# Moving four loads and one block of sums, and adding epsilon as a sum over pairs, in a fused attention and feed-forward kernel

## The chip, the cores and the metric

The kernel runs on one core of one Trainium2 chip. The metric is the device time of one execution in microseconds (us), the median of three runs. Five engines matter: TensorE (PE in the profile; its weight loads are PEld), VectorE (DVE), ScalarE (ACT), GpSimd (POOL) and SyncE (SP), whose only work here is to issue DMAs. Each engine takes its instructions strictly in the order in which they were written, and waits on semaphores for the others. DMAs issued by SP and ACT go to one kind of queue (q1, q10 in the profile), those issued by GpSimd to another (q0).

## The reference

```python
def _attn_ref(q, k, v, tau):
    q_n = q / (np.linalg.norm(q, axis=-1, keepdims=True) + 1e-06)
    k_n = k / (np.linalg.norm(k, axis=-1, keepdims=True) + 1e-06)
    scores = np.matmul(q_n, k_n.transpose(0, 1, 3, 2)) / tau
    scores = scores - np.max(scores, axis=-1, keepdims=True)
    attn = np.exp(scores)
    attn = attn / (np.sum(attn, axis=-1, keepdims=True) + 1e-09)
    return np.matmul(attn, v).astype(np.float32)

def _moe_ref(x, w_in, w_out):
    h = x @ w_in
    g = np.maximum(0.01 * h, h)
    return (g @ w_out).astype(np.float32)
```

q, k and v have shape (8, 12, 448, 64): 8 batches, 12 heads, 448 positions, 64 numbers each, in float32; tau is 0.1. The attention's output, (3584, 768) after its heads are put side by side, goes through w_in (768 x 2048), a leaky maximum, and w_out (2048 x 768).

## The kernel before, in words

**Slots, quads, units.** Work is cut into *slots* of normalisation. For the first two batches a slot is q and k of one pair of heads: slots 0 to 5 are batch 0, slots 6 to 11 batch 1. From slot 12 (`OLD`) on, slots come in twos that make a *unit*: the even one is q of two pairs of heads, the odd one k of the same two. Slots 12 and 13 are unit 0, slots 14 and 15 unit 1, slots 16 and 17 unit 2. A *quad* is four heads, so two slots of the first batches; quads 0 to 2 are batch 0, quads 3 to 5 batch 1.

**A slot's chain.** `load_qk(s)` loads it (lines 128 to 151; SP's queue but for slots 0 and 1, whose k is issued by ACT). `squares(s)` multiplies it with itself on GpSimd (L201, L208). `sums(s)` adds up the squares on VectorE (L216, L222). `roots(s)` takes the root as a logarithm and an exponential on ScalarE (L229, L230). `normalise(s)` adds epsilon on VectorE (L238), takes the reciprocal (L239) and multiplies it in (L245 for units, L255 for the first slots). `transposes(s)` turns the result: for the first slots on TensorE (L269) with a copy by VectorE (L310); for units on VectorE (L291), and when a unit's second slot is turned, six DMAs on SP's queue (L300) put it in place as qkT. `hold(x)` is a tiny copy on GpSimd (L585) that makes GpSimd wait for `normalise`, so that it doesn't start the next squares too soon. The pool of loaded tiles has four buffers, so slot s + 4 uses the buffer of slot s.

**Scores and products.** `key_tiles` (called by `scores`) makes score tiles of 128 keys by two heads on TensorE (L331) and ScalarE takes their exp (L340); `quad_tiles` does it for units (L402, exp L408). `totals(j)` sums a quad's exps over the keys with matmuls (L351) and takes the inverse on ScalarE as a logarithm and an exponential (L362, L363); `products(j, e)` multiplies them with the values (L351 too); `scale(j, e)` on VectorE (L382) writes the scaled result to xT. `attend(j)` is `totals`, two `products` and two `scale`. A quad's values come by `load_v(j)` (L162) and `load_v_rem(b)` (L170, last 64 positions of a batch's heads), both issued by GpSimd; for units it is `load_vq(g)` (L188).

**Feed-forward.** `first(c, m)` multiplies xT of chunk c with one 128-wide slice of w_in (L476), and ScalarE writes it to hT (L485); there are 16 slices. `second(c, ts, half)` multiplies hT with one half of w_out (L507); VectorE copies the result out (L518) and SP stores it (L527). One call of `second` is an *output group*. The weights are loaded by GpSimd: `load_w_in(i)`, i from 0 to 3 (L107), and `load_w_out(half)` (L113).

**The order.** All of it is written out by hand, in one list that fixes every engine's order. A loop over batch 0's slots (lines 621 to 676) comes first; a straight part (lines 687 to 744) does quad 2, the first groups of `first` and the normalisation of slots 6 to 10; a loop over `opened` (lines 750 to 790) does batch 1's remaining score tiles, quads 3 and 4, and five output groups, one for each of its five rounds; then *visits* (lines 829 to 882) do three quad tiles each, with further groups. In a round of `opened` the third number is the slot whose sums, roots and normalisation are due: 11, 12, 13, 14. In round 2 of the old order, for instance, that is slot 13, whose turning completes unit 0.

**PSUM banks.** PSUM's eight banks are dealt by age (`banks`, lines 78 to 88): a tile gets the bank that was dealt longest ago. A tile of two heads takes two banks. TensorE waits if the engine that reads the bank's former content isn't done.

**DMA semaphores.** The framework deals eight semaphores in turn to SP's and ACT's DMAs, and eight to GpSimd's. A DMA that is issued waits for the DMA eight before it of its kind to have landed, and the issuing engine waits with it.

Of the kernel before, what the change touches and what calls it, by code (L numbers as in the profile page):

```python
# [8 lines left out]
F32 = mybir.dt.float32  # L9
BF16 = mybir.dt.bfloat16  # L10
AF = mybir.ActivationFunctionType
ALU = mybir.AluOpType
AX = mybir.AxisListType
# [3 lines left out]
def kernel(  # L17
# [10 lines left out]
    nc = tc.nc  # L28
# [96 lines left out]
            x[:, 512:896].rearrange("p (h t d) -> p h t d", h=2, d=D),  # L125
        )

    def load_qk(s, engs=(nc.sync, nc.sync)):
        if s >= NSLOT:
            return  # L130
        whole = ldp.tile([128, 14 * D], F32, name="qk_h")
        if s >= OLD:
            u, which = divmod(s - OLD, 2)
            for w, pair in enumerate(UNITS[u][1]):
                b, h0 = pair // NPAIR, 2 * (pair % NPAIR)
                nc.sync.dma_start(
                    out=whole[64 * w : 64 * w + 64],
                    in_=(q, k)[which][b, h0 : h0 + 2].rearrange("h (p t) d -> (h p) (t d)", t=14),
                )
            raw[s] = whole  # L140
            return
        b, h0 = s // NPAIR, 2 * (s % NPAIR)
        q_h, k_h = halves(whole)
        engs[0].dma_start(out=q_h[:, :, 0:3], in_=main(q, b, h0, 2))
        engs[1].dma_start(out=k_h, in_=main(k, b, h0, 2))
        for i, (x, eng) in enumerate(zip((q, k), engs)):
            eng.dma_start(
                out=q_h[64 * i : 64 * i + 64, :, 3],
                in_=x[b, h0 : h0 + 2, MAIN:S].rearrange("h p d -> p h d"),
            )  # L150
        raw[s] = (q_h, k_h)
# [5 lines left out]
    def load_v(j):  # L157
        if j >= B * NQ:
            return
        b, jj = divmod(j, NQ)  # L160
        vb[j] = vbp.tile([128, 4, 3, D], BF16, name="v_b")
        gp.dma_start(out=vb[j], in_=main(v, b, 4 * jj, 4))  # L162

    def load_v_rem(b, heads=range(4)):
        if b >= B:
            return
        r = v[b, :, MAIN:S].rearrange("(j g) p d -> g p j d", g=4)
        for g in heads:
            lo = 64 * (g // 2)
            gp.dma_start(out=vrb[b % 2][lo : lo + 64, :, g], in_=r[g])  # L170
# [9 lines left out]
    def load_vq(g):  # L180
        js = GROUPS[g]
        nh = 2 * len(js)
        vq[g] = vqp.tile([128, 4, 7, D], BF16, name="vq")
        for w in range(2):
            b, jj = divmod(js[w % len(js)], NQ)
            h0 = 4 * jj + (2 * w if len(js) == 1 else 0)
            rows = slice(64 * w, 64 * w + 64)
            gp.dma_start(  # L188
                out=vq[g][rows, 0:nh],
                in_=v[b, h0 : h0 + nh].rearrange("h (p x) d -> p h x d", x=7),  # L190
            )
# [3 lines left out]
    def squares(s, engs=(gp, gp)):  # L195
        if s >= NSLOT:
            return
        sq = sqp.tile([128, 14 * D], F32, name="sq")
        if s >= OLD:
            sqs[s] = sq  # L200
            gp.tensor_tensor(sq, raw[s], raw[s], op=ALU.mult)  # L201
            return
        sqs[s] = halves(sq)
        for x, y, eng in zip(raw[s], sqs[s], engs):
            if eng is nc.scalar:
                nc.scalar.activation(y, x, func=AF.Square)
            else:
                eng.tensor_tensor(y, x, x, op=ALU.mult)  # L208
# [17 lines left out]
    def roots(s):  # L226
        if s >= NSLOT:
            return
        nc.scalar.activation(ss[s], ss[s], func=AF.Ln, bias=tiny)  # L229
        nc.scalar.activation(ss[s], ss[s], func=AF.Exp, scale=0.5)  # L230

    qn = {}

    def normalise(s):
        if s >= NSLOT:
            return
        r = smp.tile([128, 14], F32, name="r")
        nc.vector.tensor_tensor(ss[s], ss[s], eps, op=ALU.add)  # L238
        nc.vector.reciprocal(r, ss[s])  # L239
        if s >= OLD:  # L240


            qn[s] = qnp.tile([128, 7, D, 2], BF16, name="qn")
            t, n = ("(m e)", "(e m)")[s % 2], 2
            nc.vector.tensor_tensor(  # L245
                qn[s].rearrange("p m d e -> p m e d"),
                raw[s].rearrange(f"p ({t[1:-1]} d) -> p m e d", e=n, d=D),
                r.rearrange(f"p {t} -> p m e", e=n).unsqueeze(3).to_broadcast([128, 7, 2, D]),
                op=ALU.mult,
            )  # L250
            return
        qn[s] = qnp.tile([128, 7, 2, D], BF16, name="qn")
        for x, lo, hi, r0 in ((raw[s][0], 0, 4, 0), (raw[s][1], 4, 7, 8)):
            nt = hi - lo
            nc.vector.tensor_tensor(  # L255
                qn[s][:, lo:hi],
                x.rearrange("p h t d -> p t h d"),
                r[:, r0 : r0 + 2 * nt].rearrange("p (h t) -> p t h", h=2)
                .unsqueeze(3).to_broadcast([128, nt, 2, D]),
                op=ALU.mult,  # L260
            )
# [286 lines left out]
            work[c].pop(0)[1]()  # L548

    load_qk(0, (nc.sync, nc.scalar))  # L550
    load_qk(1, (nc.sync, nc.scalar))
    load_qk(2)
    load_qk(3)
    tiny = cpool.tile([128, 1], F32, name="tiny")
    nc.vector.memset(tiny, 1e-18)
    eps = cpool.tile([128, 14], F32, name="eps")
    nc.vector.memset(eps, 1e-6)
    warm = pep.tile([128, 2 * S], BF16, name="pe")[:, 0:512]
    nc.vector.memset(warm, 1.0)  # L559
    ones = cpool.tile([128, 32], BF16, name="ones")  # L560
# [60 lines left out]
    for s in range(NPAIR):  # L621
        j = s // 2 - 1 if s >= 2 else None
        even = s % 2 == 0
        n = s + 2 if 0 < s < NPAIR - 2 else None
        last = s == NPAIR - 1
        if s == 1:
            roots(2)
        scores(s, (0,))
        if j is not None and not even:
            products(j, 1)  # L630
        scores(s, (1,))
        fill(2)
        if n:
            sums(n, (0,))
        if not last:
            normalise(s + 1)
            load_qk(s + 5)
        if late:
            scale(late.pop(), 1)
        if j is not None and not even:  # L640
            scale(j, 0)
        if last:
            load_v(s // 2 + 1)
            load_v_rem(1)
            load_w_out(0)
        else:
            hold(qn[s + 1][:, 6, 0, 0:1])
        squares(s + 3)
        if s == 0:
            sums(2)  # L650
            load_v_rem(0, range(2, 4))
        if not even and not last:
            load_v(s // 2 + 1)
        if s != 1 and not last:
            load_w_in(max(s - 1, 0))
        if n:
            sums(n, (1,))
        scores(s, (2,))
        if not even or s == 0:
            fill(2)  # L660
        if n and not even:
            roots(n)
        if not even:
            scores(s, (3,))
        if j is not None and even:
            totals(j)
        if not last:
            transposes(s + 1)
        if j is not None and even:
            products(j, 0)  # L670
        if not even or s == 0:
            fill(2)
        if n and even:
            roots(n)
        if j is not None and not even:
            late.append(j)
# [24 lines left out]
    for m in range(2):  # L701
# [36 lines left out]
    transposes(s + 3)  # L738
    roots(s + 4)
    normalise(s + 4)  # L740
    load_qk(s + 7)
    hold(qn[s + 4][:, 6, 0, 0:1])
    squares(s + 5)
    feed_groups(0, 1)
# [3 lines left out]


    opened = [  # L750
        (0, [(2, 0), (2, 1), (2, 2)], 5),
        (None, [(3, 0), (3, 1), (3, 2)], 6),
        (None, [(4, 0), (4, 1), (3, 3)], 7),
        (1, [(4, 2), (5, 0), (5, 1)], 8),
        (None, [(5, 2), (5, 3)], None),
    ]
# [1 line left out]
    b = 1  # L758
    queue += work[0]
    costs = [BLOCK + (ATTEND if at is not None else 0) for at, _, _ in opened[1:] + [(2, 0, 0)]]  # L760
    for i, (at, tiles, ahead) in enumerate(opened):
        share = (sum(g[0] for g in queue[:-1]) + sum(costs[i:])) / (len(opened) - i) - costs[i]
        if at is not None:
            attend(b * NQ + at)
            if at == 0:
                load_v(b * NQ + 2)
            else:
                load_vq(0)
        key_tiles([(b * NPAIR + p, ki) for p, ki in tiles])
        done = 0  # L770
        s = b * NPAIR + ahead if ahead else NSLOT
        sums(s)
        roots(s)
        if i < 2:
            if i == 1:
                cost, fn = queue.pop(0)
                fn()
                done += cost
            transposes(NPAIR + 4 + i)
        if s < NSLOT:  # L780
            normalise(s)
            if s >= OLD:
                transposes(s)
            load_qk(s + 3)
            hold(qn[s][:, 6, 0, 0:1])
            squares(s + 1)
        while len(queue) > 1 and (i == len(opened) - 1 or done + queue[0][0] / 2 <= share):
            cost, fn = queue.pop(0)
            fn()
            done += cost  # L790
    load_qk(OLD + 6)
    sums(OLD + 3)
    squares(OLD + 4)
# [137 lines left out]
```

## Time and profile before

| what | us |
|---|---|
| median of 3 runs | 422.59 (422.2 to 422.63) |
| the profiled execution, device time | 422.44 |
| its span in the profile | 420.7 |
| TensorE busy | 410.2 |
| ScalarE busy | 254.7 |
| VectorE busy | 223.2 |
| GpSimd busy | 115.2 |
| first matmul starts | 1.51 |

The profile's page lists each engine's busy time, and groups of instructions by line, with the idle time of the engine just before them and what ended it. The trace also gives a timeline: start, duration, engine, line, operation, what is written and read, how many instructions in a row were merged (x12), and in brackets the idle time before the row with what released it, for instance `[1.30 <-DMA v_b<-in_v_dram]`. Times in the text without another word are microseconds from the span's start. A DMA's landing is its issue plus the time that the trace gives for issue to landing.

### The profile page before, as it was taken

How to read it: one execution, taken by the hardware profiler on the slowest of the kernel's cores; microseconds unless marked ns; L12 is line 12 of the kernel's file. 1: busy time of each engine (PE TensorE's matmuls, PEld its weight loads, DVE VectorE, ACT ScalarE, POOL GpSimd, SP SyncE). 2: the span in 40 equal slices, each digit the busy share in tenths (PEclk: the TensorE clock that was granted, in tenths of full speed). 3: DMA queues.
4: the chain of work that ended last, by engine and by line, in shares of the span. 5: the costliest groups of instructions: out<-in, count | busy, mean ns of one | idle time of the engine just before them, and what ended most of it. 6: DMA issues, size and time to landing. Idle time of an engine off the chain costs nothing.

```text
span 420.7 us, 11326 instructions
## 1 busy us (share of the span) xinstructions
PE 410.2 (98%) x4779; PEld 212.5 (51%) x4797; DVE 223.2 (53%) x383; ACT 254.7 (61%) x430; POOL 115.2 (27%) x149
## 2 busy tenths in 40 slices
PE   8898999999999999999999999999999999999996
PEld 3234555444455555554445555554445555654563
DVE  6885887785668745776564964565511312110021
ACT  3895885678847686658866687657764454104300
POOL 3868262533234132413331432123010000000000
PEclk9999999999999999999999999999999999999999
DMA  6899999767376953674465574543441100010021
GB/s 171 163 232 232 212 243 185 176 185 208 63 186 153 242 132 67 158 200 130 77 161 161 117 197 110 138 125 92 88 89 43 74 38 3 37 76 0 2 75 75
DMA packets 41906, 53.82 MB, mean 128 GB/s; under 512 B 12544, under 2 KB 32256, under 8 KB 41856
## 3 DMA queue, kind: packets, MB, share of 16 engines
q1 hardware_dynamic: 25536, 40.85, 34.1%
q0 software_dynamic: 15488, 11.80, 19.5%
q8 instruction: 37, 0.61, 0.6%
q10 hardware_dynamic: 832, 0.46, 0.4%
q14 instruction: 13, 0.11, 0.1%
HBM read 45.61 MB, written 11.01 MB: 135 GB/s over the span
## 4 chain that ended last, share of the span: by engine, by line
PE 92%; DMA 4%; DVE 2%; issue 1%; POOL 0%; SPq 0%; ACT 0%; POOLq 0%; DVEq 0%
PE ps L507 35%; PE ps L476 35%; PE ps L427 9%; PE ps L402 7%; PE ps L351 2%; DMA qk_h<-in_k_dram 2%; PE ps L576 2%; DMA v_b<-in_v_dram 2%; PE ps L331 1%; PE ps L269 1%; DVE qn L255 1%; POOL sq L208 0%; DVE ss L222 0%; DVE ss L238 0%; DVE osb L518 0%
## 5 line engine op out<-in xcount | busy, mean ns | idle before, releaser
L507 PE MATMUL ps<-w_out_sb,hT 128*128 128x384 bf16 x896 | 151.5, 327 | 0.2 <-DVE xT L382 0.2
L476 PE MATMUL ps<-xT,w_in_sb 128*128 128x384 bf16 (+1 forms) x753 | 149.8, 353 | 0.9 <-issue 0.2
L408 ACT ACTIVATE pe<-ps 128x896 bf16<-128x896 f32 x126 | 108.9, 916 | 41.6 <-PE ps L402 41.6
L507 PEld LDWEIGHTS <-hT 128*128 128x128 bf16 x896 | 85.3, 98 | 64.7 <-issue 10.4
L476 PEld LDWEIGHTS <-w_in_sb 128*128 128x128 bf16 x768 | 73.0, 98 | 73.5 <-issue 8.4
L485 ACT ACTIVATE hT<-ps 128x384 bf16<-128x384 f32 (+1 forms) x128 | 67.9, 548 | 63.0 <-PE ps L476 62.4
L518 DVE COPY osb<-ps 128x384 f32<-128x384 f32 (+1 forms) x56 | 30.8, 550 | 106.1 <-PE ps L507 100.4
L201 POOL TENSOR_TENSOR sq<-qk_h 128x896 f32<-128x896 f32 x36 | 60.4, 1679 | 4.8 <-DMA qk_h<-in_k_dram 2.6
L585 POOL CAST seen<-qn 128x1 f32<-128x1 bf16 x46 | 8.4, 184 | 176.2 <-DVE qn L245 161.8
L245 DVE TENSOR_TENSOR qn<-qk_h,r 128x896 bf16<-128x896 f32 x36 | 42.5, 1181 | 1.2
L340 ACT ACTIVATE pe<-ps 128x896 bf16<-128x896 f32 x42 | 36.0, 917 | 6.3 <-PE ps L331 6.3
L216 DVE TENSOR_REDUCE ss<-sq 128x14 f32<-128x896 f32 x36 | 37.5, 1041 | 2.5 <-POOL sq L201 2.5
L402 PE MATMUL ps<-qkT 64*32 64x448 bf16 x1008 | 37.0, 353 | 0.0
L238 DVE TENSOR_TENSOR ss<-ss,eps 128x14 f32<-128x14 f32 x48 | 11.0, 228 | 46.8 <-ACT ss L230 46.4
L452 DVE TENSOR_TENSOR xT<-ps,rb 128x448 bf16<-128x448 f32 x32 | 18.4, 617 | 21.9 <-PE ps L427 20.8
L291 DVE STREAM_TRANSPOSE tt<-qn 128x448 f32<-128x448 f32 x36 | 29.5, 820 | 0.9
L427 PE MATMUL ps<-pe,vq 64*32 64x448 bf16 x1008 | 27.0, 349 | 0.0
L229 ACT ACTIVATE ss<-ss,tiny 128x14 f32<-128x14 f32 x48 | 14.7, 306 | 19.1 <-DVE ss L216 16.7
L402 PEld LDWEIGHTS <-qkT 64*32 64x32 bf16 x1008 | 13.3, 91 | 20.0 <-issue 15.4
L208 POOL TENSOR_TENSOR sq<-qk_h 128x384 f32<-128x384 f32 (+1 forms) x21 | 20.1, 974 | 10.0 <-DMA qk_h<-in_k_dram 10.0
L427 PEld LDWEIGHTS <-vq 64*32 64x32 bf16 x1008 | 14.6, 93 | 7.9 <-issue 0.3
L576 PE MATMUL ps<-pe 128*128 128x512 bf16 x50 | 16.5, 454 | 1.6 <-DVE pe L559 1.5
(52 smaller groups left out, 216.0 us busy)
## 6 DMA issues: line engine op xcount, KB each, us to landing
qk_h<-in_q_dram SPq DMA_DIRECT2D x36, 224.0 KB, 4.1
qk_h<-in_k_dram SPq DMA_DIRECT2D x36, 224.0 KB, 4.4
out_dram<-osb SPq DMA_DIRECT2D x20, 384.0 KB, 2.6
qkT<-tt SPq DMA_DIRECT2D x72, 56.0 KB, 2.7
qkT<-tt SPq DMA_DIRECT2D x36, 112.0 KB, 2.9
vq<-in_v_dram POOLq DMA_DIRECT2D x16, 224.0 KB, 4.9
w_in_sb<-in_moe_w_in_dram POOLq DMA_DIRECT2D x4, 768.0 KB, 10.1
w_out_sb<-in_moe_w_out_dram POOLq DMA_DIRECT2D x2, 1536.0 KB, 20.7
```

Source lines behind the costliest of these rows:

```text
L201: gp.tensor_tensor(sq, raw[s], raw[s], op=ALU.mult)
L216: nc.vector.tensor_reduce(ss[s], sqs[s].rearrange("p (t d) -> p t d", d=D), axis=AX.X, op=ALU.add)
L245: nc.vector.tensor_tensor(qn[s].rearrange("p m d e -> p m e d"), raw[s].rearrange(f"p ({t[1:-1]} d) -> p m e d", e=n, d=D), r.rearrange(f" ...
L291: nc.vector.transpose(out=to.rearrange(("p g (c m) -> p m g c", "p g (m c) -> p m g c")[which], m=7), in_=qn[s].bitcast(F32).rearrange("p ...
L340: nc.scalar.activation(out=dst, in_=sc[:, :, :S], func=AF.Exp, scale=inv_tau)
L402: nc.tensor.matmul(out=sc[32 * strip : 32 * strip + 32, a, :S], lhsT=x[rows, c0 : c0 + 32], rhs=x[rows, 0:S], start=True, stop=True,)
L408: nc.scalar.activation(out=pq[u, i], in_=sc[:, :, :S], func=AF.Exp, scale=inv_tau)
L427: nc.tensor.matmul(out=po[32 * strip : 32 * strip + 32, w, :S], lhsT=weights, rhs=pq[us[x if two else 0], i][rows, a, :], start=(i == 0), ...
L476: nc.tensor.matmul(out=pm[:, :n], lhsT=w_in_sb[:, kt, m * 128 : (m + 1) * 128], rhs=xT[c // 2][:, kt, c0 : c0 + n], start=(kt == 0), stop= ...
L485: nc.scalar.activation(out=hT[c][:, m, :n], in_=pm[:, :n], func=AF.Prelu, alpha=0.01)
L507: nc.tensor.matmul(out=po2[:, :HALF], lhsT=hT[c][:, m, ts * 128 : (ts + 1) * 128], rhs=w_out_sb[:, m, half * HALF : (half + 1) * HALF], st ...
L518: nc.vector.tensor_copy(out=o[:, half * HALF : half * HALF + cut], in_=po2[:, :cut])
```

## The change

The first slots' loads: slot 1's last piece of k is issued by SP in place of ACT. Epsilon: the root is written next to a constant 1e-6, so that pairs (root, epsilon) lie side by side in one of three tiles, and `normalise` sums each pair, where it added two tiles. Batch 0's loop: quad 2's values are loaded in round 2 where it was round 3; in the last round the first half of w_out is loaded, and slot 8 squared, ahead of quad 3's values. The `opened` loop: quad 3's sums and products move from round 0 to round 2. In rounds 0 and 1 a slot's normalisation stays ahead of the output groups; in rounds 2 and 3 it comes behind the group. Loads 13, 14 and 15 are called one round later than they were (load 13 in round 0 in place of the straight part, and so on), and round 3 calls loads 16 and 17; `load_vq(0)` moves to the end of round 3.

In the order of instructions this comes to the following. TensorE: the sums and products of quad 3 (48 matmuls) move behind the second output group and slot 11's transposes; the first output group now stands ahead of slot 9's score tiles. SP: load 15 moves from before the first six DMAs of L300 to behind them; the first store follows it, ahead of loads 16 and 17; loads 13 and 14 keep their places. GpSimd: the loads named above, and `load_vq(0)` behind the squares of slot 15. VectorE: three memsets in place of one, and quad 3's two scalings behind slot 12's turning.

```diff
-    def load_qk(s, engs=(nc.sync, nc.sync)):
+    def load_qk(s, engs=(nc.sync, nc.sync), rem_engs=None):
...
-        for i, (x, eng) in enumerate(zip((q, k), engs)):
+        for i, (x, eng) in enumerate(zip((q, k), rem_engs or engs)):
...
         nc.scalar.activation(ss[s], ss[s], func=AF.Ln, bias=tiny)
-        nc.scalar.activation(ss[s], ss[s], func=AF.Exp, scale=0.5)
+        nc.scalar.activation(norms[s % 3][:, :, 0], ss[s], func=AF.Exp, scale=0.5)
...
-        nc.vector.tensor_tensor(ss[s], ss[s], eps, op=ALU.add)
-        nc.vector.reciprocal(r, ss[s])
+        nc.vector.tensor_reduce(r, norms[s % 3], axis=AX.X, op=ALU.add)
+        nc.vector.reciprocal(r, r)
...
-    load_qk(1, (nc.sync, nc.scalar))
+    load_qk(1, (nc.sync, nc.scalar), (nc.sync, nc.sync))
...
-    eps = cpool.tile([128, 14], F32, name="eps")
-    nc.vector.memset(eps, 1e-6)
+    norms = []
+    for i in range(3):
+        norms.append(cpool.tile([128, 14, 2], F32, name=f"norms{i}"))
+        nc.vector.memset(norms[i], 1e-6)
...
         if last:
-            load_v(s // 2 + 1)
-            load_v_rem(1)
             load_w_out(0)
...
-        if not even and not last:
-            load_v(s // 2 + 1)
-        if s != 1 and not last:
+        if s in (1, 2):
+            load_v(s)
+        if last:
+            load_v(NQ)
+            load_v_rem(1)
+        elif s != 1:
             load_w_in(max(s - 1, 0))
...
     normalise(s + 4)
-    load_qk(s + 7)
     hold(qn[s + 4][:, 6, 0, 0:1])
...
     opened = [
-        (0, [(2, 0), (2, 1), (2, 2)], 5),
+        (None, [(2, 0), (2, 1), (2, 2)], 5),
         (None, [(3, 0), (3, 1), (3, 2)], 6),
-        (None, [(4, 0), (4, 1), (3, 3)], 7),
+        (0, [(4, 0), (4, 1), (3, 3)], 7),
...
         if at is not None:
             attend(b * NQ + at)
-            if at == 0:
-                load_v(b * NQ + 2)
-            else:
-                load_vq(0)
+        if i == 0:
+            load_v(b * NQ + 2)
...
-        if s < NSLOT:
+
+        def prepare():
             normalise(s)
             if s >= OLD:
                 transposes(s)
-            load_qk(s + 3)
+            for n in ((s + 2,), (s + 2, s + 3))[i == 3]:
+                load_qk(n)
             hold(qn[s][:, 6, 0, 0:1])
             squares(s + 1)
+
+        if i < 2:
+            prepare()
         while len(queue) > 1 and (i == len(opened) - 1 or done + queue[0][0] / 2 <= share):
...
             done += cost
+        if i in (2, 3):
+            prepare()
+        if i == 3:
+            load_vq(0)
```

## The prediction

> **What bounds the kernel now.** I read four views in this order: the page's head, TensorE's timeline, the timeline of all engines from 52 to 86 us, and the DMA queue's own timeline with the bytes moved per microsecond. Times are microseconds of the one profiled execution: span 420.7, device time 422.44, which is 0.15 under the median of the three runs shown (422.59).
>
> ```profile
> span 420.7 us, 11326 instructions
> ...
> PE 410.2 (98%) x4779; PEld 212.5 (51%) x4797; DVE 223.2 (53%) x383; ACT 254.7 (61%) x430; POOL 115.2 (27%) x149
> ```
>
> TensorE (PE) is busy for 98%, and its work doesn't change: the same 9,596 rows, in which one block has moved. So the time can only move by TensorE's idle time, 10.5 us, of which 1.5 lie before its first matmul and 3.6 behind its last. What is left is 5.4, nearly all before 90 us. The two largest waits:
>
> ```profile
> 14.77 0.55 PE L331 MATMUL ps<-qkT 64*128 64x448 bf16 x4 [0.81 <-ACT ss L230]
> ...
> 36.76 0.75 PE L351 MATMUL ps<-pe,v_b 128*32 128x448 bf16 x12 [1.30 <-DMA v_b<-in_v_dram]
> ```
>
> From 38.4 to 73 TensorE never waits, yet several producers there finish only just before it comes, so an order that brings it sooner to something may open a wait. The rows that decide this case, out of the timelines of the engines (start, duration, engine, line; the rows between them are left out):
>
> ```profile
> 54.76 0.31 ACT L229 ACTIVATE ss<-ss,tiny 128x14 f32<-128x14 f32 x1 [0.36 <-DVE ss L222]
> 55.83 1.16 DVE L255 TENSOR_TENSOR qn<-qk_h,r 128x512 bf16<-128x512 f32 x2
> 57.83 0.57 PE L269 MATMUL ps<-id,qn 128*128 128x128 bf16 x7
> ...
> 62.29 1.11 SPq L136 DMA_DIRECT2D qk_h<-in_k_dram  x2
> 74.06 3.79 SPq L300 DMA_DIRECT2D qkT<-tt  x6
> 78.35 1.15 SPq L136 DMA_DIRECT2D qk_h<-in_q_dram  x2
> ...
> 81.43 1.07 DVE L216 TENSOR_REDUCE ss<-sq 128x14 f32<-128x896 f32 x1
> 82.54 0.31 ACT L229 ACTIVATE ss<-ss,tiny 128x14 f32<-128x14 f32 x1 [2.74 <-DVE ss L216]
> 82.80 1.68 POOL L201 TENSOR_TENSOR sq<-qk_h 128x896 f32<-128x896 f32 x1 [2.17 <-DMA qk_h<-in_q_dram]
> 83.00 0.90 ACT L408 ACTIVATE pe<-ps 128x896 bf16<-128x896 f32 x1
> 83.54 0.79 PE L402 MATMUL ps<-qkT 64*32 64x448 bf16 x16
> ```
>
> See three things. Slot 10's transposes (57.83) follow the end of its normalised values (56.99) by 0.84 only. Slot 15's load is issued at 62.29, and 16's, behind the six DMAs of L300, at 78.35; the squares of 16 (82.80) wait for it, 4.45 after its issue. And slot 15's roots (82.54) stand in ScalarE's queue ahead of the first exp of the quad tiles (83.00 to 83.90). The third quad tile uses that exp's two PSUM banks again, so it starts at about 84.0: 16 matmuls took 0.79 where 0.56 is usual.
>
> **The change, part by part.** Third quad's values: the load of quad 2's values moves in GpSimd's queue from 29.89 (landed 36.71, 6.82 later) to 22.80, in front of the second load of input weights. The slowest load of values near it took 8.4, so it lands by 31.2, and TensorE asks at 35.46: minus 1.30. Next late are those weights: landed 33.3 before, now behind 0.2 MB more (about 1.2 at the 0.16 MB per us that this queue moves there), so 34.5 against a need at 36.8. Nothing.
>
> Epsilon: 48 adds of two operands (L238, 0.228 mean, 0.17 the usual one) become 48 sums over pairs of 28 elements. The nearest rows are that 0.17 and the 0.278 of a sum of 128 elements; I take 0.18, VectorE being half idle, and nothing on TensorE's path. The gain is elsewhere: three of the old adds took 0.85, 0.64 and 1.39, and each ended as GpSimd's running multiplication did, while sums over 384 and 512 elements beside such multiplications took their usual time. Only the one at 10.81 is on the path: it ended at 11.66, the multiply L255 ran to 13.13, two sums and the copy L310 to 14.72, and TensorE started at 14.77. A sum ends at 11.0; the multiply has two operands and still waits for GpSimd's end at 11.63, or at about 11.3 if GpSimd too is earlier. That is 0.3 to 0.6 out of the 0.81; I take 0.4. The Trainium skill's page "SBUF — State Buffer", section "SBUF: two separate sides", says that VectorE and GpSimd take a shared port pair as an exclusive lock held for the whole instruction, an operation with two SBUF inputs among those that need it. By that rule the lock isn't removed, only handed to the next multiply; the trace agrees (2.00 and 2.02 for the pair of L255 at 27.25 and 51.43, where 1.16 is usual), and the sum by it is the 0.3. Against this, two more memsets stand before the one that TensorE's first matmul waits for (eps to it: 0.13 start to start). Between 0.06 and 0.26; I take 0.1. Start-up together: minus 0.3.
>
> Slot 1's last piece of k goes from ScalarE's queue to SP's: it waited there from 2.62 to 5.38, and ScalarE's first square started at 6.02 though q had landed at 3.83. Roots of slot 0 could come 1.3 sooner, but VectorE has a sum there that waits for GpSimd until 6.99, and TensorE warms up until 9.40 in any case. On SP the k of slot 2 then waits for a landing at 5.34 in place of 4.25; its squares start at 9.8. Nothing.
>
> Output weights ahead of later values: POOL issues the first half at about 33.5 in place of 37.39, and its queue no longer has quad 3's values (landed 45.05, remainders 45.9, the load ahead of them 44.16: 1.74) in front. It landed at 60.9 and was used at 61.95. Now output groups begin before key tiles (0.69) and quad 3's sums (2.38), at 58.83 of the old clock, which the other terms shift to 58.2. Landing by the 1.74 alone is 59.2; the queue also stood nearly empty from 31.5 to 33.2 (8 of 589 packets in one us), which the earlier values fill: 58.0. Between 0 and 1.0 late; I take 0. Quad 3's values land behind them, at about 60, and are wanted at 66; the four remainder loads hold POOL from about 37 to 40, before slot 6's hold. Nothing.
>
> Fourth quad's sums later (attend(3), 2.38): TensorE comes to slot 10's transposes at 55.52 of the old clock, not 57.83. What they wait for doesn't move with the block: ScalarE is free for slot 10's roots at 54.39 (end of L485), 0.37 sooner than it did them. From the roots' start to the ends of the two multiplies it took 1.76 and 2.23: 56.16 and 56.63. The last three of seven transposes follow the second, and end at 56.9 in place of 55.91: plus 1.0. Low end 0.6 (first multiply alone), high end 1.6 (VectorE lost 0.86 at 51.43 beside GpSimd's squares of slot 10, which depend on a load that landed at 51.8).
>
> The moved block also puts its two scalings (L382) on VectorE behind slot 12's normalisation. The third output group takes a PSUM bank that the first scaling frees. From the copy at 65.21 to the end of slot 12's transpose was 3.51, the scaling is 0.62, the sum 4.2 from the second group's end; TensorE arrives after 0.39 + 2.38 + 0.69 = 3.46. Plus 0.75 (0.3 to 1.0).
>
> Norms behind output groups, and loads with them: slot 13's normalisation now follows the third group's copy, and load 15 (62.29 before) follows on SP the six L300 of the unit that slot 13 completes. Count from the third group's end, 71.11 before. Copy, add, reciprocal, multiply, transpose: 0.04 + 0.47 + 0.20 + 0.27 + 1.26 + 0.65 = 2.89, and 0.13 to L300: 3.02. Six L300 3.79: load 15 at 6.9. Squares 4.45 later, as for slot 16: 11.35, and 1.67 long. Sum starts at 13.05, roots 1.11 later (81.43 to 82.54): 14.16; from there to the end of the exp 1.36: 15.5. Third quad tile at 15.6, where it was 84.0 - 71.11 = 12.9. Plus 2.7. A quiet load took 3.0 to land; with 0.57 between its two DMAs that gives 0.9 less, and load 19's squares came 4.89 behind its issue, 0.4 more: 1.8 to 3.1. Behind it ScalarE holds the exp and the logs of quad 5, but the tile covers them. Slot 15's own transposed tiles then land at 24.4 on this count and are wanted at 24.7. The values for group 0 move from 75.14 to behind squares 15 and are wanted at 108. Loads 13 and 14 keep their place on SP.
>
> Sum: -1.30 - 0.3 + 1.0 + 0.75 + 2.7 = +2.85, so 422.44 + 2.85 = 425.3.
>
> **The rivals.** (1) Faster: the waits at the values and in start-up go, and no new one opens: -1.6, 420.8. It needs three covers at once in slots 10, 12 and 15, but one decides: slot 15's squares must start within 8.6 of the third group's end, not 11.35, so load 15 must be issued 2.7 sooner. SP's order speaks against it (six L300, then load 15); for it speaks only that landing times here run from 2 to 10. (2) Slot 15 is in time, the two smaller waits remain: -1.6 + 1.75 = +0.15, 422.6: the change buys nothing. (3) The output weights are late by the whole 1.0 too: 426.3. For it: the queue's tail was starved from 55.5 to 58.5 (39 packets a us against 160) by loads of 3.5 KB rows beside it. The Trainium skill's page "DMA: Bandwidth & Descriptors", section "Queues, rings and completion order", says each DMA engine goes round robin between queues by packet; the trace agrees (153 and 153 packets in the microsecond from 46), and by it a queue loses to larger packets just as seen, wherever its transfer still has a tail at 55.
>
> **How the numbers follow.** Forecast, slot 15 late: 0.64. Rival 1: 0.12. Rival 2: 0.10, half of it within 0.2% (0.84 us, about what a measurement of this kernel can tell from no change), 0.04 slower, 0.01 faster. Rival 3: 0.14. Slower 0.64 + 0.14 + 0.04 = 0.82, same 0.05, faster 0.13. Low ends of all terms (0.6, 0.3, 1.8) give 423.5, high ends with the weights 422.44 - 1.6 + 1.6 + 1.0 + 3.1 + 1.0 = 427.5, unlikely together. 422.5 to 426.5 leaves out rival 1, part of rival 2 and the top of rival 3, some 0.19; the forecast's own range is 423.5 to 426.5.
>
> **What would show it.** No wait for v_b at the third quad; L238 at 0.17 to 0.28 and never over 0.4; a wait of about 1 before slot 10's transposes (L269); one of about 0.75 before the third output group, released by L382; load 15 on SP right behind the first six L300; GpSimd's squares of slot 15 waiting for that load; ScalarE's roots of slot 15 idle for over 4 us; and TensorE idle for some 2.7 in the middle of visit 0, released by L408. I am wrong if load 15 has landed before GpSimd comes to it, or if the quad tile finds its banks free.

## The result, and the profile after

The changed kernel takes 429.06 us (median of 4 runs, 428.32 to 429.84) against 422.61 before: a ratio of 1.0155, 95% interval 1.0133 to 1.0177. It is slower, as forecast, but by 6.5 us and not by 2.7; 429.06 lies outside the range of 422.5 to 426.5. The profiled execution took 429.49 us, with a span of 427.7, 7.0 longer than the span before. One run of the epsilon kernel below (1484.48 us) and one of the kernel before that ran beside the last four kernels (704.23 us, mean clock 0.559) were slow ones and are in no median or ratio here.

The head of the profile and the row of the granted clock, of the kernel after:

```profile
PE 412.0 (96%) x4779; PEld 213.0 (50%) x4797; DVE 222.3 (52%) x385; ACT 255.2 (60%) x430; POOL 116.7 (27%) x149
...
PEclk9999999969999999999999999999999999999999
```

The same row of the clock before, and the sixth output group in TensorE's timeline before:

```profile
PEclk9999999999999999999999999999999999999999
...
84.26 2.77 PE L507 MATMUL ps<-w_out_sb,hT 128*128 128x384 bf16 x16
```

TensorE's busy time has grown by 1.8 although its work is the same, and one slice of the 40, the one from about 86 us on, was granted a clock of only 0.6. Before, every slice of that row read 9. Next, TensorE's own timeline after (start, duration, engine, line, operation, instructions; idle time ahead and what ended it):

```profile
14.49 0.55 PE L331 MATMUL ps<-qkT 64*128 64x448 bf16 x4 [0.62 <-ACT norms L230]
...
35.04 0.74 PE L351 MATMUL ps<-pe,v_b 128*32 128x448 bf16 x12
...
53.81 0.94 PE L331 MATMUL ps<-qkT 64*64 64x448 bf16 x12
55.64 0.81 PE L269 MATMUL ps<-id,qn 128*128 128x128 bf16 x7 [0.89 <-DVE qn L255]
...
69.65 2.76 PE L507 MATMUL ps<-w_out_sb,hT 128*128 128x384 bf16 x16 [0.81 <-DVE xT L382]
72.34 0.75 PE L351 MATMUL ps<-pe,ones 128*32 128x448 bf16 x12
...
84.47 0.38 PE L402 MATMUL ps<-qkT 64*32 64x448 bf16 x8
88.34 0.57 PE L402 MATMUL ps<-qkT 64*32 64x448 bf16 x8 [3.48 <-ACT pe L408]
88.84 5.30 PE L507 MATMUL ps<-w_out_sb,hT 128*128 128x384 bf16 x16
```

The wait for quad 2's values is gone (35.04), and the three waits of the forecast are there: 0.89 at slot 10's transposes, 0.81 at the third output group, 3.48 at the third quad tile. What is new is the row behind it: an output group of 16 matmuls takes 5.30, where the five ahead of it took 2.76 or 2.77, as it did itself before. The clock says why, here in windows of the trace after (stretch, its length, busy time and instructions of PE, PEld, DVE, ACT and POOL, then the granted clock, the DMA share and GB/s):

```profile
87.00:88.00 1.00, 0.00 (x0) 0.00 (x0) 0.42 (x2) 0.97 (x3) 0.00 (x0) 0.68 0.99 280
88.00:89.00 1.00, 0.66 (x9) 0.25 (x9) 0.99 (x1) 0.97 (x3) 0.83 (x1) 0.50 1.07 359
...
94.00:95.00 1.00, 0.86 (x25) 0.37 (x26) 0.78 (x3) 0.43 (x1) 0.00 (x0) 0.91 0.35 84
```

TensorE's last matmul ends at 84.85 (84.47 + 0.38). Some 2.5 later, while it still waits, the clock falls to 0.50, and it stays there through the whole output group. A difference table of the two profiles, by the start of the same block of TensorE's work, shows where the 7.0 arose:

| block of TensorE | before | after | behind by |
|---|---|---|---|
| input group behind quad 2's products (L476) | 38.38 | 36.66 | -1.72 |
| input group behind slot 9's transposes (L476) | 53.69 | 52.75 | -0.94 |
| sums behind the third output group (L351) | 71.04 | 72.34 | +1.30 |
| sixth output group (L507) | 84.26 | 88.84 | +4.58 |
| key tiles behind it (L402) | 86.97 | 94.07 | +7.10 |

From there on the two run alike. The stall itself can be followed in the timeline of all engines after, from the loads of SP to TensorE:

```profile
75.45 3.77 SPq L300 DMA_DIRECT2D qkT<-tt  x6
...
79.34 1.16 SPq L136 DMA_DIRECT2D qk_h<-in_k_dram  x2
...
84.09 1.68 POOL L201 TENSOR_TENSOR sq<-qk_h 128x896 f32<-128x896 f32 x1 [2.98 <-DMA qk_h<-in_k_dram]
...
85.81 1.09 DVE L216 TENSOR_REDUCE ss<-sq 128x14 f32<-128x896 f32 x1 [3.37 <-POOL sq L201]
86.93 0.31 ACT L229 ACTIVATE ss<-ss,tiny 128x14 f32<-128x14 f32 x1 [6.20 <-DVE ss L216]
...
87.39 0.90 ACT L408 ACTIVATE pe<-ps 128x896 bf16<-128x896 f32 x1
```

Load 15 goes out at 79.34 in place of 62.29, right behind the six L300. GpSimd waits 2.98 for it, ScalarE's roots of slot 15 wait 6.20, and the exp (L408) that would free TensorE's banks stands behind those roots.

### The profile page after: what moved, and what is told of

It is laid out like the page before. It is cut to its first block, busy times and chain, and to the rows that moved or that the text cites. A ratio compares the mean times of both kernels' runs of the same rounds, so it can differ in the third digit from the quotient of the medians.

```text
span 427.7 us, 11313 instructions
## 1 busy us (share of the span) xinstructions
PE 412.0 (96%) x4779; PEld 213.0 (50%) x4797; DVE 222.3 (52%) x385; ACT 255.2 (60%) x430; POOL 116.7 (27%) x149
## 3 DMA queue, kind: packets, MB, share of 16 engines
q1 hardware_dynamic: 25680, 40.88, 34.3%
## 4 chain that ended last, share of the span: by engine, by line
PE 85%; DMA 5%; DVE 4%; ACT 2%; SPq 1%; issue 1%; POOL 1%; ACTq 0%; POOLq 0%; DVEq 0%
PE ps L507 34%; PE ps L476 31%; PE ps L427 9%; PE ps L402 7%; DMA qk_h<-in_q_dram 3%; DMA qk_h<-in_k_dram 2%; DVE qn L255 1%; PE ps L351 1%; PE ps L331 1%; SPq L300 1%; PE ps L269 1%; PE ps L578 1%; ACT pe L340 1%; DVE qn L245 1%; DVE qkT L310 0%
## 5 line engine op out<-in xcount | busy, mean ns | idle before, releaser
L507 PE MATMUL ps<-w_out_sb,hT 128*128 128x384 bf16 x896 | 154.0, 330 | 1.2 <-DVE xT L382 1.2
L476 PE MATMUL ps<-xT,w_in_sb 128*128 128x384 bf16 (+1 forms) x753 | 149.8, 352 | 0.9 <-issue 0.2
L408 ACT ACTIVATE pe<-ps 128x896 bf16<-128x896 f32 x126 | 109.0, 916 | 43.5 <-PE ps L402 43.5
L507 PEld LDWEIGHTS <-hT 128*128 128x128 bf16 x896 | 86.2, 99 | 67.6 <-issue 14.2
L476 PEld LDWEIGHTS <-w_in_sb 128*128 128x128 bf16 x768 | 73.1, 98 | 73.5 <-issue 8.4
L402 PE MATMUL ps<-qkT 64*32 64x448 bf16 x1008 | 37.1, 354 | 3.5 <-ACT pe L408 3.5
L216 DVE TENSOR_REDUCE ss<-sq 128x14 f32<-128x896 f32 x36 | 37.5, 1042 | 4.0 <-POOL sq L201 4.0
L238 DVE TENSOR_REDUCE r<-norms 128x14 f32<-128x28 f32 x48 | 8.6, 179 | 46.6 <-ACT norms L230 46.2
L402 PEld LDWEIGHTS <-qkT 64*32 64x32 bf16 x1008 | 13.1, 91 | 23.9 <-issue 18.8
L255 DVE TENSOR_TENSOR qn<-qk_h,r 128x512 bf16<-128x512 f32 (+1 forms) x24 | 17.0, 748 | 0.4
```

The lines of the kernel that those rows point to most:

```text
L216: nc.vector.tensor_reduce(ss[s], sqs[s].rearrange("p (t d) -> p t d", d=D), axis=AX.X, op=ALU.add)
L402: nc.tensor.matmul(out=sc[32 * strip : 32 * strip + 32, a, :S], lhsT=x[rows, c0 : c0 + 32], rhs=x[rows, 0:S], start=True, stop=True,)
L408: nc.scalar.activation(out=pq[u, i], in_=sc[:, :, :S], func=AF.Exp, scale=inv_tau)
L476: nc.tensor.matmul(out=pm[:, :n], lhsT=w_in_sb[:, kt, m * 128 : (m + 1) * 128], rhs=xT[c // 2][:, kt, c0 : c0 + n], start=(kt == 0), stop= ...
L507: nc.tensor.matmul(out=po2[:, :HALF], lhsT=hT[c][:, m, ts * 128 : (ts + 1) * 128], rhs=w_out_sb[:, m, half * HALF : (half + 1) * HALF], st ...
```

## The experiments

**The load put back.** In the changed kernel, only slot 15's load goes out one round sooner:

```diff
-            for n in ((s + 2,), (s + 2, s + 3))[i == 3]:
+            for n in ((s + 2,), (s + 2, s + 3), (), (s + 2, s + 3))[i]:
                 load_qk(n)
```

> The changed kernel with one thing undone: slot 15's load is issued one round sooner, ahead of the first six DMAs of L300 on SP (as in the kernel before) instead of behind them. Theory (the load's new place on SP starves GpSimd's squares of slot 15, its roots hold ScalarE's exp, TensorE idles 3.48 us ahead of the third quad tile, and its clock then falls to 0.50, so that the sixth output group takes 5.30 instead of 2.77): wait gone, sixth group 2.77, 429.06 - 3.48 - 2.53 = 423.0, between 422.7 and 423.6; what stays over the kernel before are the waits at slots 8 to 10 and at the scaling (L382). Rival (slot 13's normalisation, moved behind the third output group, is what is late, and the load only lands beside it): the wait stays at 3 or more, 428 to 429. Rival (the sixth group is slow by itself, for instance beside the DMAs of L300): wait gone, group still 5.3, 425.6.

Measured: 424.02 us, ratio to before 1.0036 (1.0022 to 1.0050), so about 5 of the 6.5 us are gone. TensorE's timeline of this kernel:

```profile
86.09 0.38 PE L402 MATMUL ps<-qkT 64*32 64x448 bf16 x8 [0.46 <-ACT pe L408]
86.41 2.77 PE L507 MATMUL ps<-w_out_sb,hT 128*128 128x384 bf16 x16
```

The stall shrank from 3.48 to 0.46 and the group takes 2.77 again, so the load's place on SP is the cause of both. The time missed the expected 423.0 by 1.0: 0.46 of that is the wait that stayed, and another 0.43 comes from taking durations of the profiled execution (429.49) off the median (429.06).

**TensorE kept busy.** The stall stays, but useless matmuls fill it:

```diff
-        quad_tiles(tiles[1:])
+        quad_tiles(tiles[1:2])
+        if n == 0:
+            for i in range(11):
+                nc.tensor.matmul(
+                    out=ps[:, 1], lhsT=w_in_sb[:, 0, 0:128], rhs=w_in_sb[:, 0, 0:512],
+                    start=(i == 0), stop=(i == 10),
+                )
+        quad_tiles(tiles[2:])
```

> The changed kernel with 11 more matmuls (512 columns each, some 2.4 us in all) between the second and the third quad tile of the first visit; they fill the 3.48 us in which TensorE waits there, and what they compute is used nowhere. Theory (the idle time itself takes the clock down): the third quad tile starts no sooner (about 16.0 after the third group's end), but the granted clock stays at 1.0 and the sixth output group takes 2.77: 429.06 - 2.53 = 426.5, between 426.2 and 427.0. Rival (the sixth group is slow because its operands or its weight loads are held up by other traffic): it takes 5.3 again, 429.1 or a little more. The Trainium skill's page TensorE: Matmul & The Clock Gate, section Part 1: The HAM clock gate, says that the clock is halved after an idle window of about 3.4 us; by that page the theory holds here, since what is left of the wait is about 1 us.

Measured: 426.79 us, ratio 1.0104 (1.0088 to 1.0119). This kernel does more work than the changed one and is faster than it (429.06, and 428.40 in the later comparison). TensorE's timeline (L868 is the added work):

```profile
85.19 2.55 PE L868 MATMUL ps<-w_in_sb 128*128 128x512 bf16 x11
88.32 0.38 PE L402 MATMUL ps<-qkT 64*32 64x448 bf16 x8 [0.58 <-ACT pe L408]
88.63 2.77 PE L507 MATMUL ps<-w_out_sb,hT 128*128 128x384 bf16 x16
```

The third quad tile starts where it did (88.32 against 88.34), with the same loads issued, but every window from 82 to 94 us has a clock of 1.00 and the group takes 2.77. All four runs have a mean clock of 0.999 or 1.000, and their median lies between the two runs of the changed kernel in which the clock held (426.20 and 426.93, in the table below). So the idle time takes the clock down, not the traffic beside it.

**The late load alone.** In the kernel before, only slot 15's load is moved behind the six L300:

```diff
-            load_qk(s + 3)
+            for n in ((s + 3,), (), (s + 2, s + 3), (s + 3,), ())[i]:
+                load_qk(n)
```

> The kernel before with one thing changed: slot 15's load is issued behind the first six DMAs of L300 on SP (those begin at 74.06 there and take 3.79) instead of at 62.29. Theory (this alone makes the stall): load at 77.9, squares 4.45 later, 82.3 to 84.0, sum 1.07, roots, exp: third quad tile at about 87.0 instead of 84.0, plus 3.0, so 425.6; if the idle time of 3 us is enough to take the clock down, another 2.5: 428.1. Rival (it takes the moved norms and sums too): plus 0 to 1, 422.6 to 423.6.

Measured: 427.28 us, ratio 1.0116 (1.0099 to 1.0134), +4.85 over the 422.43 of before in the same comparison. Its profiled execution (428.11) in TensorE's timeline:

```profile
87.06 0.58 PE L402 MATMUL ps<-qkT 64*32 64x448 bf16 x8 [3.29 <-ACT pe L408]
87.57 5.24 PE L507 MATMUL ps<-w_out_sb,hT 128*128 128x384 bf16 x16
```

The third quad tile comes at 87.06, where 87.0 was worked out, and the slow group follows. This one line of the change makes three quarters of its loss (4.85 of 6.45).

**The norms behind the output groups alone.** In the kernel before, slots 13 and 14 are normalised behind their rounds' groups, and the loads keep their order:

```diff
-        if s < NSLOT:
+        def prepare():
             normalise(s)
...
+        if i < 2:
+            prepare()
         while len(queue) > 1 and (i == len(opened) - 1 or done + queue[0][0] / 2 <= share):
...
+        if i in (2, 3):
+            prepare()
```

> The kernel before with one thing changed: the normalisation, transposes, load, hold and squares of slots 13 and 14 stand behind their round's output groups; slot 15's load keeps its place at about 62.3. Theory (the norms' place costs nothing as long as the load is early): within 0.5 of 422.6, the third quad tile at about 84, no drop of the clock. Rival (the norms behind the groups are themselves the cause: L300 some 1.4 later, roots of slot 15 or 16 later, exp held): plus 1.5 to 6, 424 to 428.6.

Measured: 422.51 us, ratio 0.9999 (0.9989 to 1.0008). The norms' place costs nothing; its rival is out.

**The values alone.** In the kernel before:

```diff
-        if not even and not last:
-            load_v(s // 2 + 1)
+        if s in (1, 2):
+            load_v(s)
```

> The kernel before with one thing changed: quad 2's values are loaded one round sooner, ahead of the second load of input weights. Theory (the 1.30 wait goes, and part of it comes back, since with GpSimd's loads sooner the SP loads of slots 8 and 9 land later, at 38.6 and 43 to 45 in the changed kernel where it was 34.3 and 37.5, and TensorE then waits 0.4 to 0.9 before their transposes): 422.43 - 0.5 to 0.9 = 421.5 to 421.9. Rival (those loads are pushed back by the output weights that go ahead, not by the values): no wait at slots 8 and 9, the full 1.3 to 1.6: 420.8 to 421.1. Rival (nothing is gained): 422.4.

Measured: 422.17 us, ratio 1.0003 (0.9990 to 1.0016): no gain, though the wait for v_b is gone. The gain can be seen to go in two rows of its timelines, GpSimd's and TensorE's:

```profile
44.75 1.82 POOL L208 TENSOR_TENSOR sq<-qk_h 128x512 f32<-128x512 f32 x2 [3.89 <-DMA qk_h<-in_k_dram]
...
61.91 2.77 PE L507 MATMUL ps<-w_out_sb,hT 128*128 128x384 bf16 x16 [1.34 <-DMA w_out_sb<-in_moe_w_out_dram]
```

Slot 9's load, issued at the same time as before (29.3 to 31.5), now lands at 44.7 in place of 37.5, and its squares wait 3.89; that, as expected, does happen, but TensorE has no wait at slots 8 and 9. It waits where I had not looked for it: at the output weights. They are issued 1.8 sooner (35.57 against 37.39) and land no sooner (61.9 against 60.9). The first output group starts at 61.91; before, it started at 61.95. In the kernel before those weights had 1.05 to spare. In the seven profiled executions here that leave them behind quad 3's values and remainders they landed between 60.5 and 61.9, though they were issued anywhere from 35.6 to 38.8; so while they stay there, a gain ahead of them is worth 1.5 us at best (61.95 - 60.48).

**The epsilon alone.** In the kernel before:

```diff
-        nc.scalar.activation(ss[s], ss[s], func=AF.Exp, scale=0.5)
+        nc.scalar.activation(norms[s % 3][:, :, 0], ss[s], func=AF.Exp, scale=0.5)
...
-        nc.vector.tensor_tensor(ss[s], ss[s], eps, op=ALU.add)
-        nc.vector.reciprocal(r, ss[s])
+        nc.vector.tensor_reduce(r, norms[s % 3], axis=AX.X, op=ALU.add)
+        nc.vector.reciprocal(r, r)
```

> The kernel before with one thing changed: the norms' epsilon is added as a sum over pairs. Theory: the add that waited for GpSimd goes (0.228 mean becomes 0.18), the start-up is 0.3 shorter: 422.1. Rival (the port is only handed on to the next multiply, or another input of the start-up is late instead): 422.4, no difference that can be told.

Measured: 422.00 us (median of 11 runs), ratio 0.9992 (0.9981 to 1.0004), no difference that can be told. In its timeline TensorE's start-up wait is the 0.81 that it was:

```profile
14.80 0.55 PE L331 MATMUL ps<-qkT 64*128 64x448 bf16 x4 [0.81 <-ACT norms L230]
```

**The sums later, alone.** In the kernel before, only attend(quad 3) moves from round 0 to round 2:

```diff
-        (0, [(2, 0), (2, 1), (2, 2)], 5),
+        (None, [(2, 0), (2, 1), (2, 2)], 5),
...
-        (None, [(4, 0), (4, 1), (3, 3)], 7),
+        (0, [(4, 0), (4, 1), (3, 3)], 7),
```

> The kernel before with one thing changed: the fourth quad's sums stand in round 2, not round 0; norms, loads of slots 13 to 16 and weights keep their places. Theory: a wait of about 0.9 to 1.0 ahead of slot 10's transposes, one of 0.75 at the third output group (L382), and, as the output weights land at about 60.9 and are asked for at 59.8, another of about 1: 425.2; without the last 424.2. The third quad tile waits for less than 0.5 and the clock stays at 1.0. Rival (the moved sums alone bring on the stall of 3.5 at the third quad tile): 427 or more. Rival (they cost nothing, TensorE's other work covers them): 422.4.

Measured: 424.04 us, ratio 1.0037 (1.0025 to 1.0050), +1.7. TensorE's timeline:

```profile
56.65 0.81 PE L269 MATMUL ps<-id,qn 128*128 128x128 bf16 x7 [0.89 <-DVE qn L255]
...
60.70 2.77 PE L507 MATMUL ps<-w_out_sb,hT 128*128 128x384 bf16 x16 [0.33 <-ACT hT L485]
...
71.14 2.76 PE L507 MATMUL ps<-w_out_sb,hT 128*128 128x384 bf16 x16 [0.80 <-DVE xT L382]
```

Both waits are there at the sizes of the forecast, and the stall is not. The expected wait for the output weights is there too, but small: it is the 0.33 ahead of the first output group. The row names hT, but the weights land at 60.7 (38.40 + 22.3), when the group starts, and the row of TensorE's weight loads beside it shows 0.71 of waiting for them.

**The two that could pay, together.** Values and epsilon, in the kernel before, by the edits shown:

> The kernel before with only the two parts that could pay: quad 2's values one round sooner, and epsilon as a sum over pairs. Theory: the sum of the two single runs, 422.43 - 0.3 - 0.7 = 421.4, a kernel faster than both. Rival (the earlier start makes the loads of slots 8 and 9 the limit, so that the second gain buys nothing): 421.7 or more.

Measured: 422.15 us (421.45 to 424.2), ratio 1.0000 (0.9986 to 1.0014). Its profiled execution (421.63) had no wait for the output weights and a span 0.8 shorter than the one before, but its runs spread over more than that. Its longest run, 424.2, has a mean clock of 0.995, the others 0.998 to 1.000. The rival stands: no gain.

**The first half of the change.** Everything up to the rounds as changed, the rounds as before. The edit, as what is taken back from the change:

```diff
-        (None, [(2, 0), (2, 1), (2, 2)], 5),
+        (0, [(2, 0), (2, 1), (2, 2)], 5),
...
-        (0, [(4, 0), (4, 1), (3, 3)], 7),
+        (None, [(4, 0), (4, 1), (3, 3)], 7),
...
-            for n in ((s + 2,), (s + 2, s + 3))[i == 3]:
-                load_qk(n)
+            load_qk(s + 3)
```

> The change up to the rounds of the first visit (values sooner, epsilon over pairs, output weights ahead of the fourth quad's values, slot 1's last piece on SP); sums, norms and loads of the rounds as in the kernel before. Theory (values alone gained nothing since the output weights landed at 61.9 and became the wait; weights ahead take that away): the lead of 0.9 that the changed kernel still had ahead of slot 10 stays to the end, 422.4 - 0.9 = 421.5. Rival (the loads of slots 8 to 10, pushed back by both, take all of it): 422.2 to 422.6.

Measured: 429.32 us, ratio 1.0184 (1.0154 to 1.0214). Theory and rival both fell. TensorE's timeline of it:

```profile
60.59 1.31 PE L351 MATMUL ps<-pe,v_b 128*32 128x448 bf16 x12 [5.63 <-DMA v_b<-in_v_dram]
```

and GpSimd's timeline:

```profile
38.72 2.17 POOL L208 TENSOR_TENSOR sq<-qk_h 128x512 f32<-128x512 f32 x2 [4.92 <-DMA qk_h<-in_k_dram]
40.83 0.82 POOL L162 DMA_DIRECT2D v_b<-in_v_dram  x1
```

With the output weights (1536 KB, issued at 32.61) ahead, quad 3's values go out at 40.83 only, since GpSimd's own squares of slot 8 stand between and wait 4.92 for their load. They land at 60.5; the sums of quad 3, back in round 0, want them at 55. TensorE idles 5.63, and the clock falls here too: these 12 matmuls took 1.31 in place of 0.74. So two parts of the change depend on each other: the weights can go ahead only because the sums come later, and the sums' 1.7 is paid for that.

**Values and weights only.** As the first half, without the epsilon and slot 1's load; the edit is the change's own, cut here to its core:

```diff
         if last:
-            load_v(s // 2 + 1)
-            load_v_rem(1)
             load_w_out(0)
...
+        if s in (1, 2):
+            load_v(s)
+        if last:
+            load_v(NQ)
+            load_v_rem(1)
```

> The kernel before with quad 2's values sooner and the output weights ahead of the fourth quad's values; no other part. Theory: as the first half without the start-up's part, 421.7 (between 421.3 and 422.0). Rival (the weights were not the limit, the loads of slots 8 and 9 are): 422.2 to 422.6.

Measured: 430.16 us, ratio 1.0173 (1.0152 to 1.0194), with 6.72 of waiting for the same v_b.

**The weights between.** As the first half, with the output weights behind quad 3's values and ahead of their remainders:

```diff
         if last:
+            load_v(NQ)
             load_w_out(0)
+            load_v_rem(1)
```

> As the first half of the change, but the output weights go behind the fourth quad's values and ahead of their remainders. Theory (ahead of everything they press on the loads of slots 8 and 9; here they are issued about 0.8 later and still land by 60): 421.3 to 421.6, no wait at slots 8 and 9 over 0.4 and none for the weights. Rival (the place makes no difference to those loads): as the first half.

Measured: 429.55 us, ratio 1.0173 (1.0159 to 1.0186). The values are in time now, and the remainders take their place in TensorE's timeline:

```profile
60.98 1.27 PE L351 MATMUL ps<-pe,v_rem 128*32 128x448 bf16 x4 [5.44 <-DMA v_rem<-in_v_dram]
```

In the changed kernel and in these three, the load next behind those 1536 KB on GpSimd's queue landed between 60.5 and 61.6.

**The changed kernel again**, beside the last three:

> The changed kernel itself, run again beside the others. Theory (the clock is set by windows of fixed length, so that the half clock lasts 6.8 in one run and half of that, 3.4, in another): every run's mean clock is near 0.992 or near 0.996, and the runs at 0.992 are 1.2 to 1.5 longer than those at 0.996 (429.5 to 429.8 against 428.3 to 428.6 so far). Rival (the fall follows the length of the idle time): clocks and times spread evenly between.

Measured: 428.40 us (426.2 to 430.04), ratio 1.0137 (1.0108 to 1.0166). All ten runs of the changed kernel, by the mean clock of the run:

| mean clock | times (us) | mean |
|---|---|---|
| 0.999 to 1.000 | 426.93, 426.20 | 426.6 |
| 0.995 to 0.996 | 428.62, 428.32, 428.15, 429.42 | 428.6 |
| 0.992 | 429.49, 429.84, 428.65, 430.04 | 429.5 |

A mean of 0.992 over 427.7 us is 3.4 us of lost clock, or 6.8 at 0.50; 0.996 is half of that. I had expected the two lower rows, and not the first: in two runs of ten the clock did not fall at all. The groups are there and their times follow them, but they overlap (429.42, 428.65), so the step of 1.2 to 1.5 was too neat.

## Why the prediction was wrong

- **The stall at the third quad tile: right in place, cause and size.** Counted from the third group's end (69.65 + 2.76 = 72.41), load 15 was issued at 6.9 (forecast 6.9), the squares began at 11.7 (11.35), the tile at 15.9 (15.6). The row of SP's order decided it, as the first rival's condition had said.
- **The failed step is the price put on that stall: "Third quad tile at 15.6, where it was 84.0 - 71.11 = 12.9. Plus 2.7."** It took the idle time for the whole cost and let the work behind it run at its old durations. The idle time was 3.48, and the group behind it cost 2.53 more at half clock; load 15 alone, predicted at 2.7, measured 4.85. No term of the sum and no rival had the clock in it, so no range made of them could reach 429. The two runs in which the clock held, 426.2 and 426.9, lie on either side of the range's upper end.
- **The gains, mis-sized: minus 1.30 and minus 0.3.** Both showed in the first 38 us (-1.72). By slot 9 only 0.94 was left in the profiled execution (0.50 and 1.41 in those of the kernel kept busy and of the changed kernel again, whose orders are the same up to there): the loads of slots 8 and 9 landed at 38.6 and 45.5 (34.3 and 37.5 before), with GpSimd's loads now in flight beside them, and the transposes of slot 8 waited 0.37 for VectorE's multiplies. The values alone put slot 9's load at 44.7; that the rest comes from the loads beside it too is argued, not shown. I had followed the moved load to its own landing and that of the weights behind it ("Nothing"), and not to the loads of the other queue. The start-up term of 0.3 wasn't found by its own run (0.9992): the wait is 0.81 in all six profiled executions with the old form; of the eight with the new form, five have 0.62 to 0.68, two have 0.81 and one none. The sums themselves came as forecast (L238 at 0.17 to 0.18), and the two more memsets put the first matmul at 1.60 in place of 1.51 (0.1 forecast).
- **Sums later: right.** 1.0 and 0.75 forecast; the waits in brackets are 0.89 and 0.81. By the starts of the rows the first costs more, since the last of slot 10's transposes waited within their own row: from the score tiles ahead of them to the input group behind them it took 2.48 (53.81 to 56.29), before 1.09, so 1.4; the second costs 0.9 (1.57 for 0.69). Both lie in the forecast's bounds. Alone, the move measured +1.7.
- **Output weights: right for the whole change, by a cover I hadn't priced.** They landed at 57.1 (58.0 forecast), and quad 3's values at 60.7 (about 60), wanted at 66 only because the sums had moved. Undone alone, that cover is worth 5.6 of idle time.
- **Sum of the single parts:** 4.85 (load) + 1.7 (sums) + 0 (norms) + about 0 (values, epsilon) = 6.5; the whole change measured 6.45, and 6.1 in the second comparison (428.40 against 422.32, the median of ten runs). As the medians of the load and of the whole change are over runs with one and with two losses of the clock, a match to 0.1 is partly luck. No version here beat the kernel before: the best ratios, 0.9992 and 1.0000, can't be told from 1. What spreads the runs of values and epsilon over 1.9 us, leaving out the one at 424.2, stays open.
- **Two sums of its working are off by little:** TensorE's rows are 4779 + 4797 = 9,576 and not 9,596, and the output groups would begin at 61.95 - 0.69 - 2.38 = 58.88, not 58.83. Nothing rests on either.

## What to carry to other kernels

When a change opens an idle time of about 3 us (3.16 to 3.48 here) on a TensorE that was busy without a break, price it with the clock: the idle time and then up to another 2.5 us of the work behind it. Follow a moved transfer not only to its own landing but to those of every queue that was in flight beside it, and to whatever stands behind it in its own queue. And try a part of a change together with the parts that cover it: the output weights ahead, which cost nothing in the whole change, cost 7.0 us (429.32 against 422.32) without the sums that moved with them.

## What the runs showed of the hardware

In the six profiled executions in which it came at a long wait, the half clock lasted the same time. In quarter-microsecond windows of the trace after, the fall and the rise (columns as above; the clock is the third number from the end):

```profile
87.25:87.50 0.25, 0.00 (x0) 0.00 (x0) 0.00 (x0) 0.23 (x2) 0.00 (x0) 0.73 1.04 277
...
94.00:94.25 0.25, 0.25 (x9) 0.15 (x16) 0.07 (x1) 0.00 (x0) 0.00 (x0) 0.62 0.13 29
```

and of the kernel with load 15 late alone:

```profile
85.75:86.00 0.25, 0.00 (x0) 0.00 (x0) 0.00 (x0) 0.22 (x2) 0.25 (x1) 0.58 1.01 395
...
92.50:92.75 0.25, 0.25 (x5) 0.01 (x4) 0.00 (x0) 0.00 (x0) 0.00 (x0) 0.77 0.60 144
```

A slice at 0.73 was at full clock for 0.46 of itself, so the clock fell at 87.36 and rose at 94.19: 6.83 us. In the second trace it is 85.79 to 92.61: 6.82. The fall came 2.5 and 2.0 after TensorE's last matmul (84.85 and 83.77), the rise 5.9 and 5.6 after work began again. The same windows of four more traces (the changed kernel again, first half, values and weights, weights between) give 6.82 or 6.83 each, for waits of 3.16, 5.63, 6.72 and 5.44, with the fall 2.2 to 3.7 after the last matmul and the rise 3.7 to 5.9 after work began again. A stretch of half that length stands in the start-up of the kernel with the load put back, in its windows:

```profile
11.00:12.00 1.00, 1.00 (x6) 0.13 (x2) 0.87 (x3) 0.80 (x2) 1.00 (x3) 0.56 0.56 143
...
14.00:15.00 1.00, 1.00 (x9) 0.60 (x6) 0.29 (x1) 0.52 (x2) 1.00 (x3) 0.73 0.81 98
```

There the clock was halved from 11.12 to 14.54, 3.42 us, after TensorE had idled for 1.60 up to 9.44 and had been at work again for 1.7; that this gap caused it is not shown. With the ten runs above all this fits a clock that is decided in steps of about 3.4 us whose phase against the kernel differs from run to run: none, one or two steps at half clock for the same kernel. The idle time is on record for two of the ten only, both with two steps (3.16 and 3.48), so that it was much the same in the others is assumed. The Trainium skill's page "TensorE: Matmul & The Clock Gate", section "Part 1: The HAM clock gate", describes such a free-running window of about 3.4 us and gives an idle window of that length as the condition of the fall; the length agrees with these traces, but a fall after 2.0 us without a matmul is sooner than that condition says, and the measurement decides. Other gaps near 1.60, of 1.12 to 1.74 at v_b and 1.34 at the output weights, left the clock at 1.0 in their profiled executions.
